# V's global rows copied on VectorE, one values tile fewer, and a rewoven first tile in a windowed-attention and SwiGLU kernel

## The chip, the cores and the metric

The kernel runs on one core of a Trainium2 chip. The metric is the device time of one execution in microseconds (us). The engines are TensorE (PE; its weight loads are listed apart as PEld), VectorE (DVE), ScalarE (ACT), GpSimd (POOL) and SyncE (SP). Each works through its own instructions in program order, and they wait for one another through semaphores. DMA transfers are issued from POOL, SP or ACT and run beside the engines.

## The reference

Attention with a local window and global keys, then a SwiGLU block. There are 4 batches, 8 heads, 768 positions, head size 64, 8 global keys and a window of 96.

```python
scores = scale * np.matmul(q, k.transpose(0, 1, 3, 2))
is_global = pos[None, :] < 8
is_local = (rel >= 0) & (rel < 96)              # rel = query position - key position
keep = is_global | is_local
dist = np.where(is_global & ~is_local, 96.0, np.abs(rel))
scores = np.where(keep, scores - slopes[:, None, None] * dist, -1e9)
a = softmax(scores)
x = np.matmul(a, v)                             # then heads side by side: 3072 x 512
# SwiGLU: d_model 512, d_ff 1536
g = x @ w_gate
out = (g * sigmoid(g) * (x @ w_val)) @ w_out
```

## The kernel before

Keys are taken in chunks of 120 beside the 8 global keys, so that a chunk fills 128 rows: rows 0 to 7 hold the global keys, rows 8 to 127 the chunk's own. `vS0` to `vS3` hold V of the four batches in that form, seven chunks each. A batch's 768 queries are worked in two halves of 384 (`TB`); each half becomes one tile of the SwiGLU block (`t` = 0 to 7). Half 0 of batch 0 needs chunks 0 to 2 and the first 24 keys (`cut`) of chunk 3. For these 24 keys the kernel before has a tile of its own, `vCut`, whose other rows are zero.

```python
vSs = [sb.tile([128, NCH, H, D], FP16, name=f"vS{b}") for b in range(B)]
...
for b in range(B):
    nc.vector.memset(vSs[b][:, 6, :, :], 0.0)
cut = TB - 3 * KC                                   # 24
vCut = sb.tile([128, H, D], FP16, name="vCut")
nc.vector.memset(vCut, 0.0)
...
def copy_globals(b):                                # global rows into all seven chunks, by DMA
    nc.sync.dma_start(
        out=vSs[b][0:NG],
        in_=vG[:, b, :, :].unsqueeze(1).broadcast_to([NG, NCH, H, D]))

def load_v_rest(b, c):                              # a chunk's own rows; casts to fp16 (L171)
    n = min(KC, S - KC * c)
    nc.gpsimd.dma_start(
        out=vSs[b][NG:NG + n, c, :, :],
        in_=v[b, :, KC * c:KC * c + n, :].rearrange("h p d -> p h d"))
```

A quad is four heads. `weigh` makes the denominators (with ones) or the numerators (with V) of a half in one PSUM bank (L447):

```python
def weigh(self, half, dst, side):
    parts = self.parts(half)
    for i, (c, cb, col, o, n) in enumerate(parts):
        vals = vCut if (b, half, c) == (0, 0, 3) else vSs[b][:, c]
        for j in range(4):
            nc.tensor.matmul(
                dst[r, o:o + n],
                lhsT=ones[:, 0:32] if side is None else vals[:, 4 * g + j, side::2],
                rhs=pairs[b, 2 * g + j // 2].at[cb][:, j % 2, col:col + n], ...)
```

The start of the program, in its order:

```python
for c in range(3):
    load_v_rest(0, c)
nc.gpsimd.dma_start(
    out=vCut[NG:NG + cut], in_=v[0, :, 3 * KC:TB, :].rearrange("h p d -> p h d"))
...                                                 # warm-up, first transposes, biases
V(out=vG[:, 0], in_=vG32)
copy_globals(0)
nc.sync.dma_start(out=vCut[0:NG], in_=vG[:, 0])
load_w(wg, 0)
load_half(1, 0, 4)
load_w(wv, 0)
load_half(1, 4, 8)
load_w(wg, 4)
load_w(wv, 4)
for c in range(3, NCH):
    load_v_rest(0, c)
load_w(wg, 8)
load_w(wv, 8)
load_wo(0)
...                                                 # further loads
p_sc(0, 0)                                          # scores of half 0
...
quads[0, 0].denominators(single("den", "x2"))
p_sc(3, 1, "x0", "x1")
for side, tag in enumerate(("a0", "a1")):
    quads[0, 0].numerators(side, single("num", tag))
quads[0, 1].denominators(single("den", "o0"))
for side, tag in enumerate(("x2", "x0")):
    quads[0, 1].numerators(side, single("num", tag))
```

Tile 0 of the SwiGLU block then runs between the parts of half 1's attention. `(f, 0)` is a gate product of 128 columns of d_ff (four matmuls, L555, then tanh on ScalarE and a product on VectorE), `(f, 1)` a value product (four matmuls, then a product on VectorE). `trh` transposes half 1's keys and queries of two pairs of heads, `sch` makes a pair's biases, scores and exponentials, `va` and `vas` the numerators. Four banks `a0` to `a3` hold the first four gates, and then the biases and scores; the spare banks `x0` to `x2` go round. Some operations of VectorE and ScalarE are put into a list, `later`, and taken from it one at a time.

```python
first_gates(0, 2)                                   # matmuls of gates 0 to 3, contraction chunks 0, 1
trh(0, 1, A)()
first_gates(2, 3)
first_gates(3, 4)
tile0 = [(0, 0), (1, 0), (2, 0), (3, 0), (0, 1), (1, 1), sch(0),
         (2, 1), (3, 1), sch(1), trh(2, 3, V), (4, 0), (5, 0), sch(2), (4, 1), (5, 1),
         (6, 0), (6, 1), sch(3), (7, 0), (7, 1), va(0, 0, 1), (8, 0), (8, 1), va(0, 1, 1)]
```

Of the kernel before, what the change touches and what calls it, by code (L numbers as in the profile page):

```python
# [10 lines left out]
FP16 = mybir.dt.float16  # L11
# [4 lines left out]
KC = 120  # L16
WIN = 216
# [3 lines left out]
def _build_dist(S, NG, NL):  # L21


    row = np.arange(128)[:, None]
    col = np.arange(WIN)[None, :]
    key = row - NG
    rel = col - key
    local = (rel >= 0) & (rel < NL) & (key >= 0)
    inner = np.where(local, rel, FAR)
    inner = np.where((row < NG) & (col < KC), NL, inner)  # L30
    first = np.where(local, rel, FAR)
    first = np.where(~local & (key >= 0) & (key < NG) & (col < KC), NL, first)
    d = np.concatenate([first, inner, inner[:, :168], inner[:, :48]], axis=1)
    return d.astype(np.float16)


# [1 line left out]
def kernel(  # L38
# [12 lines left out]
    nc = tc.nc  # L51

    B, H, S, D = q.shape
    NG, NL = int(n_global), int(n_local)
# [7 lines left out]
    NC = DM // 128  # L62
    J = S // 128
    NCH = 7
    TB = 384
# [24 lines left out]
    sb = ctx.enter_context(tc.tile_pool(name="sb", bufs=1))  # L90
# [18 lines left out]
    vG32 = sb.tile([NG, H, D], FP32, name="vG32")  # L109
    nc.sync.dma_start(out=k32, in_=half_of(k, 0, 0, 2))  # L110
    nc.scalar.dma_start(out=ident, in_=const_dr.ap()[:, 0:128])
    nc.scalar.dma_start(out=dist[:, 0:2 * WIN], in_=const_dr.ap()[:, 128:128 + 2 * WIN])
    nc.sync.dma_start(out=q32, in_=half_of(q, 0, 0, 2))
    nc.sync.dma_start(out=vG32, in_=v[0, :, 0:NG, :].rearrange("h p d -> p h d"))
    nc.sync.dma_start(out=dist[:, 2 * WIN:], in_=const_dr.ap()[:, 128 + 2 * WIN:])

    def load_half(half, h0, h1):
        for st, src in ((k16, k), (q16, q)):
# [14 lines left out]
    for b in range(B):  # L133
        nc.vector.memset(vSs[b][:, 6, :, :], 0.0)
    cut = TB - 3 * KC
    vCut = sb.tile([128, H, D], FP16, name="vCut")
    nc.vector.memset(vCut, 0.0)

    slopeI = sb.tile([128, H, 128], FP16, name="slopeI")

# [41 lines left out]
                out=dst.rearrange("p b h d -> p (b h) d"),  # L182
                in_=src[1:, :, 0:NG, :].rearrange("b h p d -> p (b h) d"))

    def copy_globals(b):
        nc.sync.dma_start(
            out=vSs[b][0:NG],
            in_=vG[:, b, :, :].unsqueeze(1).broadcast_to([NG, NCH, H, D]))


    def load_rows(b, i, h):
# [228 lines left out]
    class Quad:  # L420
# [19 lines left out]
        def weigh(self, half, dst, side):  # L440
            b, g = self.b, self.g
            parts = self.parts(half)
            for i, (c, cb, col, o, n) in enumerate(parts):
                vals = vCut if (b, half, c) == (0, 0, 3) else vSs[b][:, c]
                for j in range(4):
                    r = slice(32 * j, 32 * j + 32)
                    nc.tensor.matmul(  # L447
                        dst[r, o:o + n],
                        lhsT=ones[:, 0:32] if side is None else vals[:, 4 * g + j, side::2],
                        rhs=pairs[b, 2 * g + j // 2].at[cb][:, j % 2, col:col + n],  # L450
                        start=(i == 0), stop=(i == len(parts) - 1),
                        skip_group_check=True)
# [55 lines left out]
    def both_values(b, half):  # L508
        two = [quads[b, g] for g in range(2)]
        for quad in two:  # L510
            den = spare("den")
            quad.weigh(half, den, None)
            quad.invert(den)
        srcs = {}
        for g, quad in enumerate(two):
            for side in range(2):
                num = bank("num")
                quad.weigh(half, num, side)
                src = sb2.tile([128, TB], FP32, name="ns", tag="ns", bufs=4)
                nc.scalar.copy(out=src, in_=num[:, 0:TB])  # L520
                srcs[g, side] = src

        def scale_num(eng, g, side):
            eng.tensor_mul(two[g].x_out(half, side), srcs[g, side], two[g].rb)  # L524

        def spread_first():
            two[0].spread()
            for side in range(2):
                scale_num(nc.gpsimd, 0, side)

        later.append(spread_first)
        def spread():
            two[1].spread()

        later.append(spread)
        for side in range(2):
            def scale(side=side):
                scale_num(nc.vector, 1, side)

            later.append(scale)  # L540
# [5 lines left out]
    def products(t, f, which, c0, c1, dst=None):  # L546
        if f == 0 and which == 0 and c0 == 0:
            hTs[t] = sb2.tile([128, NFF, TB], FP16, name="hT", tag="hT", bufs=3)
        if c0 == 0:
            if dst is None:  # L550
                dst = spare("gv"[which] + "ps")
            gv[f, which] = dst
        w = (wg, wv)[which]
        for c in range(c0, c1):
            nc.tensor.matmul(  # L555
                gv[f, which][:, 0:TB], lhsT=w[:, c, 128 * f:128 * f + 128],
                rhs=x_of(t)[:, c, :],
                start=(c == 0), stop=(c == NC - 1))

    def gate_or_val(t, f, which, c0=0):  # L560
        products(t, f, which, c0, NC)
        dst = gv.pop((f, which))

        if which == 0:
            th = sb2.tile([128, TB], FP32, name="th", tag="th")
            nc.scalar.activation(out=th, in_=dst[:, 0:TB], func=AF.Tanh, scale=0.5)  # L566
            if t == 0 and f < 4:
                sl = sb2.tile([128, TB], FP32, name="sl", tag="ns", bufs=4)
            else:
                sl = sb2.tile([128, TB], FP32, name="sl", tag="sl")  # L570
            nc.vector.scalar_tensor_tensor(  # L571
                out=sl, in0=th, scalar=1.0, in1=dst[:, 0:TB], op0=AluOp.add, op1=AluOp.mult)
            gv["sl", f] = sl
        else:
            nc.vector.tensor_mul(hTs[t][:, f, :], dst[:, 0:TB], gv.pop(("sl", f)))  # L575
# [37 lines left out]
    for c in range(3):  # L613
        load_v_rest(0, c)
    nc.gpsimd.dma_start(
        out=vCut[NG:NG + cut], in_=v[0, :, 3 * KC:TB, :].rearrange("h p d -> p h d"))

    warm = single("warm", "o0")

# [37 lines left out]
        make_slope(nc.vector.tensor_scalar_mul, h)  # L657
    p_tr(1, "x2", "o0", A)
    V(out=vG[:, 0], in_=vG32)
    copy_globals(0)  # L660
    nc.sync.dma_start(out=vCut[0:NG], in_=vG[:, 0])
    load_w(wg, 0)
    load_half(1, 0, 4)
    load_w(wv, 0)
# [41 lines left out]
    def first_gates(c0, c1):  # L706
        for f in range(4):
            products(0, f, 0, c0, c1, hb[f])
# [17 lines left out]
    def va(b, g, half):  # L726
        return lambda: quads[b, g].values(half, bank, nc.vector)

    def vas(b, half):
        return lambda: both_values(b, half)  # L730
# [4 lines left out]
    def trh(h0, h1, last):  # L735
        def step():
            b0, b1 = single("trs", "o0", FP16), spare("trs", FP16)
            (a, b), (c, d) = [(t[:, 0:TB], t[:, TB:2 * TB]) for t in (b0, b1)]
            pair_of = [(h0, (c, a)), (h1, (d, b))]
            for hp, tr in pair_of:  # L740
                pairs[0, hp].turn_half(1, tr)
            for hp, tr in pair_of:
                pairs[0, hp].copy_half(1, tr, V, A if hp == h0 else last)
        return step

    def sch(hp):
        def step():
            p = pairs[0, hp]
            scs = [p.bias(1, 0), p.bias(1, 1)]
            for which in range(2):  # L750
                p.scores_half(1, which, scs[which], which == 1 and hp != 1)
        return step
# [9 lines left out]
    def first(t, b):  # L762
        return {(t, 2): [tr(b, 0), tr(b, 1)],
                (t, 4): [sc(b, (0, 0), (0, 1), (1, 0))],
                (t, 5): [tr(b, 2), tr(b, 3)],
                (t, 6): [sc(b, (1, 1), (2, 0), (2, 1))],
                (t, 8): [sc(b, (3, 0), (3, 1))],
                (t, 9): [va(b, 0, 0)],
                (t, 10, 1): [va(b, 1, 0), lambda: run_later(len(later))]}
# [11 lines left out]
    def second(t, b):  # L781
        return {(t, 0): [sc(b, (0, 2), (1, 2))], (t, 3): [sc(b, (2, 2), (3, 2))],
                (t, 7): [vas(b, 1)]}

    first_gates(0, 2)
    trh(0, 1, A)()
    first_gates(2, 3)
    first_gates(3, 4)
    tile0 = [(0, 0), (1, 0), (2, 0), (3, 0), (0, 1), (1, 1), sch(0),
             (2, 1), (3, 1), sch(1), trh(2, 3, V), (4, 0), (5, 0), sch(2), (4, 1), (5, 1),  # L790
             (6, 0), (6, 1), sch(3), (7, 0), (7, 1), va(0, 0, 1), (8, 0), (8, 1), va(0, 1, 1)]

    def ff(t, f0, f1, n_out=(0,)):
        return [(t, f, n_out[(f - f0) % len(n_out)]) for f in range(f0, f1)]

    stretches = [
        (ff(0, 9, 10) + ff(0, 10, 12, (1,)), {}),
        (ff(1, 0, 4, (1, 0, 0, 1)) + ff(1, 4, 10, (1,)) + ff(1, 10, 12, (2,)), first(1, 1)),
        (ff(2, 0, 12, (1,)) + ff(3, 0, 12, (1,)), both(2, 1)),
        (ff(4, 0, 12, (1,)) + ff(5, 0, 12, (1,)), both(4, 2)),  # L800
        (ff(6, 0, 12, (1,)), second(6, 3)),
# [49 lines left out]
    for item in tile0:  # L851
        if callable(item):
            take([item])
            continue
        f, which = item
        run_later(1)
        gate_or_val(0, f, which, NC if f < 4 and which == 0 else 0)
        for fn in after.pop((0, f, which), []):
            fn()

# [60 lines left out]
```

## Time and profile before

| | |
|---|---|
| device time, median of 3 runs | 242.91 us (242.16 to 243.01) |
| span of the profiled execution | 240.4 us |
| TensorE busy | 233.6 us |
| VectorE busy | 167.0 us |
| ScalarE busy | 127.7 us |
| GpSimd busy | 94.0 us |
| moved by DMA | 25.10 MB |

The busy times show which engine has the least room. A wait is listed with the engine and line that waited, what released it, the total in us, how often, and the longest. The timeline lists instructions by start and length; in brackets stands the idle time before one and what ended it. Lines that begin with L are lines of the kernel before: L171 loads a chunk of V, L186 copies global rows by DMA, L447 makes numerators and denominators, L555 the gate and value products, L571 the product after the tanh, L347 the biases and L358 the scores of batch 0.

### The profile page before, as it was taken

Reading aid. Unit: us, or ns where it says so; the run is one execution under the profiler, and the core shown is the slowest. Engines: PE = TensorE matmul, PEld = TensorE weight load, DVE = VectorE, ACT = ScalarE, POOL = GpSimd, SP = SyncE. Lnnn points to the kernel's source line nnn. Section 1 sums busy time; section 2 is a strip of 40 time slices with the busy share of each in tenths; the row PEclk is TensorE's granted clock in tenths of the full one; section 3 lists DMA queues with packets and bytes.
Section 4 is the critical chain, followed back from the end, with each engine's and each line's share of the span. In section 5 each row is a group of like instructions: output and inputs, shape, how many; then the busy total and the mean of one; then the engine's idle time right before and its main releaser. Section 6 shows DMA issues by size and latency. Waiting matters only on the chain.

```text
span 240.4 us, 6040 instructions
## 1 busy us (share of the span) xinstructions
PE 233.6 (97%) x2424; PEld 135.5 (56%) x2424; DVE 167.0 (69%) x362; ACT 127.7 (53%) x288; POOL 94.0 (39%) x113
## 2 busy tenths in 40 slices
PE   7979999999999999999999999999999999999994
PEld 4554665656555556555555556555655556555543
DVE  6687669878897668777786668776785668555530
ACT  4826767887855374376355374376356435233311
POOL 8976574757970002995072252700031223000000
PEclk9999999999999999999999999999999999999999
DMA  7999999999996537999129749930110110111022
GB/s 144 171 200 201 182 204 205 196 165 160 153 140 103 134 80 122 111 136 122 44 57 104 128 109 131 118 64 0 48 44 3 44 44 3 46 44 45 2 88 87
DMA packets 83524, 25.10 MB, mean 104 GB/s; under 512 B 72752, under 2 KB 80552, under 8 KB 83496
## 3 DMA queue, kind: packets, MB, share of 16 engines
q0 software_dynamic: 64208, 14.05, 66.2%
q1 hardware_dynamic: 18856, 10.39, 17.6%
q8 instruction: 19, 0.31, 0.5%
q10 hardware_dynamic: 432, 0.27, 0.4%
q14 instruction: 9, 0.07, 0.1%
HBM read 28.67 MB, written 6.29 MB: 145 GB/s over the span
## 4 chain that ended last, share of the span: by engine, by line
PE 90%; POOL 4%; DMA 3%; ACT 1%; DVE 1%; issue 0%; ACTq 0%; POOLq 0%
PE gps L555 26%; PE vps L555 25%; PE ops L587 25%; PE sc L387 3%; PE num L447 3%; DMA q<-in_q_dram 3%; PE den L447 2%; PE trs L274 1%; POOL vS L171 1%; PE ops L603 1%; POOL k L119 1%; PE sc L347 1%; PE sc L358 1%; DVE sl L571 1%; ACT th L566 1%; PE trs L300 1%
## 5 line engine op out<-in xcount | busy, mean ns | idle before, releaser
L571 DVE SCALAR_TENSOR_TENSOR sl<-th,gps 128x384 f32<-128x384 f32 x96 | 52.7, 552 | 37.3 <-ACT th L566 36.6
L566 ACT ACTIVATE th<-gps 128x384 f32<-128x384 f32 x96 | 47.4, 495 | 58.7 <-PE gps L555 52.8
L555 PE MATMUL vps<-xT,wv 128*128 128x384 f16 x384 | 77.9, 326 | 0.2 <-DMA wv<-in_moe_w_val_dram 0.2
L555 PE MATMUL gps<-xT,wg 128*128 128x384 f16 x384 | 77.9, 327 | 0.0
L587 PE MATMUL ops<-wo,hT 128*128 128x512 f16 x276 | 73.3, 379 | 0.0
L575 DVE TENSOR_TENSOR hT<-vps,sl 128x384 f16<-128x384 f32 x96 | 53.1, 554 | 9.6 <-PE vps L555 1.3
L555 PEld LDWEIGHTS <-wg 128*128 128x128 f16 x384 | 35.4, 98 | 31.1 <-issue 1.6
L555 PEld LDWEIGHTS <-wv 128*128 128x128 f16 x384 | 37.2, 98 | 25.8 <-DMA wv<-in_moe_w_val_dram 0.9
L587 PEld LDWEIGHTS <-hT 128*128 128x128 f16 x276 | 26.9, 98 | 23.5
L395 ACT ACTIVATE at<-sc 128x432 f16<-128x432 f32 x72 | 33.9, 532 | 10.8 <-PE sc L387 10.8
L524 POOL TENSOR_TENSOR xT<-ns,rb 128x384 f16<-128x384 f32 x10 | 9.8, 994 | 66.6 <-DVE rb L463 55.7
L171 POOL DMA_DIRECT2D vS<-in_v_dram x28 | 24.7, 898 | 5.4 <-DMA wo<-in_moe_w_out_dram 1.5
L593 ACT ACTIVATE osb<-ops 128x512 f32<-128x512 f32 x23 | 13.7, 598 | 13.8 <-PE ops L587 13.6
L406 POOL TENSOR_TENSOR at<-at,masks 128x864 f16<-128x864 f16 x4 | 7.3, 1822 | 23.9 <-ACT at L395 19.3
L406 DVE TENSOR_TENSOR at<-at,masks 128x864 f16<-128x864 f16 x20 | 12.2, 609 | 5.2 <-ACT at L395 5.2
L194 POOL DMA_DIRECT2D kst<-in_k_dram x16 | 14.1, 897 | 2.9 <-DMA vS<-in_v_dram 1.8
L194 POOL DMA_DIRECT2D qst<-in_q_dram x16 | 13.8, 890 | 0.2 <-issue 0.2
L369 ACT ACTIVATE at<-sc 128x432 f16<-128x432 f32 (+2 forms) x32 | 11.3, 458 | 3.4 <-PE sc L358 3.4
L520 ACT COPY ns<-num 128x384 f32<-128x384 f32 x20 | 8.1, 493 | 9.3 <-PE num L447 9.3
L447 PE MATMUL num<-at,vS 128*32 128x216 f16 (+6 forms) x560 | 11.2, 226 | 1.2 <-DMA vS<-vG 1.2
L403 DVE TENSOR_TENSOR at<-at,masks 128x432 f16<-128x432 f16 x24 | 8.1, 378 | 4.0 <-ACT at L395 4.0
L457 DVE STREAM_TRANSPOSE dT<-den 128x384 f32<-128x384 f32 x16 | 9.3, 580 | 1.6 <-PE den L447 1.0
(69 smaller groups left out, 167.9 us busy)
## 6 DMA issues: line engine op xcount, KB each, us to landing
out_dram<-osb SPq DMA_DIRECT2D x23, 256.0 KB
vS<-in_v_dram POOLq DMA_DIRECT2D x24, 120.0 KB, 5.4
wg<-in_moe_w_gate_dram POOLq DMA_DIRECT2D x6, 256.0 KB, 7.7
wv<-in_moe_w_val_dram POOLq DMA_DIRECT2D x6, 256.0 KB, 7.8
wo<-in_moe_w_out_dram POOLq DMA_DIRECT2D x4, 384.0 KB, 10.0
qst<-in_q_dram POOLq DMA_DIRECT2D x16, 96.0 KB, 4.2
kst<-in_k_dram POOLq DMA_DIRECT2D x16, 90.0 KB, 4.6
kst<-in_k_dram POOLq DMA_DIRECT2D x2, 384.0 KB, 11.7
```

The costliest lines, as they stand in the source:

```text
L171: nc.gpsimd.dma_start(out=vSs[b][NG:NG + n, c, :, :], in_=v[b, :, KC * c:KC * c + n, :].rearrange("h p d -> p h d"))
L194: nc.gpsimd.dma_start(out=st[b][p0:p0 + n, h // 2, :, h % 2, :], in_=src[b, h, 0:n * J].rearrange("(t p) d -> p t d", p=n))
L369: nc.scalar.activation(out=at[:, hi, 0:col + n], in_=sc[hi][:, 0:col + n], func=AF.Exp, scale=scale)
L395: nc.scalar.activation(out=at[:, hi, :], in_=sc[hi][:, 0:BANK], func=AF.Exp, scale=scale)
L406: mul_eng.tensor_mul(at, at, m[:, :, o:o + BANK])
L447: nc.tensor.matmul(dst[r, o:o + n], lhsT=ones[:, 0:32] if side is None else vals[:, 4 * g + j, side::2], rhs=pairs[b, 2 * g + j // 2].at[c ...
L555: nc.tensor.matmul(gv[f, which][:, 0:TB], lhsT=w[:, c, 128 * f:128 * f + 128], rhs=x_of(t)[:, c, :], start=(c == 0), stop=(c == NC - 1))
L566: nc.scalar.activation(out=th, in_=dst[:, 0:TB], func=AF.Tanh, scale=0.5)
L571: nc.vector.scalar_tensor_tensor(out=sl, in0=th, scalar=1.0, in1=dst[:, 0:TB], op0=AluOp.add, op1=AluOp.mult)
L575: nc.vector.tensor_mul(hTs[t][:, f, :], dst[:, 0:TB], gv.pop(("sl", f)))
L587: nc.tensor.matmul(ops, lhsT=hTs[t][:, f, 128 * i:128 * i + 128], rhs=wo[:, f, :], start=(f == 0), stop=(f == NFF - 1))
L593: nc.scalar.mul(out=osb, in_=ops, mul=0.5)
```

## The change

The change has four parts. The global rows of V go into chunks 0 to 3 of batch 0 by a copy on VectorE, and by DMA into chunks 4 to 6 only. `vCut` is dropped: the 24 keys are loaded into `vS0`'s chunk 3, which is set to zero first, and half 0 reads that chunk. The order of tile 0 is woven anew, with the biases of pair 0 and the first half of two value products between the gates, and half 1's numerators in one group (`vas`) instead of two. The distance table is loaded without its repeated last part, which is copied on VectorE. The aim is to spare the numerators a wait for a DMA copy, to fill gaps of TensorE and to load less at the start.

```diff
-    d = np.concatenate([first, inner, inner[:, :168], inner[:, :48]], axis=1)
+    d = np.concatenate([first, inner], axis=1)
...
-    nc.scalar.dma_start(out=dist[:, 0:2 * WIN], in_=const_dr.ap()[:, 128:128 + 2 * WIN])
+    nc.scalar.dma_start(out=dist[:, 0:2 * WIN], in_=const_dr.ap()[:, 128:])
...
-    nc.sync.dma_start(out=dist[:, 2 * WIN:], in_=const_dr.ap()[:, 128 + 2 * WIN:])
...
-    vCut = sb.tile([128, H, D], FP16, name="vCut")
-    nc.vector.memset(vCut, 0.0)
+    nc.vector.memset(vSs[0][:, 3, :, :], 0.0)
...
-    def copy_globals(b):
+    def copy_globals(b, c0=0):
         nc.sync.dma_start(
-            out=vSs[b][0:NG],
-            in_=vG[:, b, :, :].unsqueeze(1).broadcast_to([NG, NCH, H, D]))
+            out=vSs[b][0:NG, c0:],
+            in_=vG[:, b, :, :].unsqueeze(1).broadcast_to([NG, NCH - c0, H, D]))
...
-                vals = vCut if (b, half, c) == (0, 0, 3) else vSs[b][:, c]
+                vals = vSs[b][:, c]
...
-                scale_num(nc.gpsimd, 0, side)
+                scale_num(nc.gpsimd if b > 0 else nc.vector, 0, side)
...
     nc.gpsimd.dma_start(
-        out=vCut[NG:NG + cut], in_=v[0, :, 3 * KC:TB, :].rearrange("h p d -> p h d"))
+        out=vSs[0][NG:NG + cut, 3], in_=v[0, :, 3 * KC:TB, :].rearrange("h p d -> p h d"))
...
     V(out=vG[:, 0], in_=vG32)
-    copy_globals(0)
-    nc.sync.dma_start(out=vCut[0:NG], in_=vG[:, 0])
+    V(out=vSs[0][0:NG, 0:4], in_=vG[:, 0].unsqueeze(1).broadcast_to([NG, 4, H, D]))
+    copy_globals(0, 4)
     load_w(wg, 0)
...
+    def bias_of(hp, which): ...      # the biases of half 1 for one pair, one score group
+    def scores_of(hp): ...           # the scores onto these biases, and the exponentials
+    def first_val(f):
+        return lambda: products(0, f, 1, 0, 2)      # value product f, contraction chunks 0, 1
+
+    V(out=dist[:, 2 * WIN:2 * WIN + 168], in_=dist[:, WIN:WIN + 168])
+    V(out=dist[:, 2 * WIN + 168:], in_=dist[:, WIN:WIN + 48])
     first_gates(0, 2)
-    trh(0, 1, A)()
     first_gates(2, 3)
     first_gates(3, 4)
-    tile0 = [(0, 0), (1, 0), (2, 0), (3, 0), (0, 1), (1, 1), sch(0),
-             (2, 1), (3, 1), sch(1), trh(2, 3, V), (4, 0), (5, 0), sch(2), (4, 1), (5, 1),
-             (6, 0), (6, 1), sch(3), (7, 0), (7, 1), va(0, 0, 1), (8, 0), (8, 1), va(0, 1, 1)]
+    tile0 = [(0, 0), (1, 0), (2, 0), (3, 0), trh(0, 1, A), bias_of(0, 0), first_val(0),
+             first_val(1), bias_of(0, 1), (0, 1), (1, 1), scores_of(0), (2, 1),
+             trh(2, 3, V), sch(1), (3, 1), sch(2), (4, 0), (5, 0), (4, 1), (5, 1),
+             (6, 0), (6, 1), sch(3), (7, 0), (7, 1), (8, 0), vas(0, 1), (8, 1)]
...
-        (ff(1, 0, 4, (1, 0, 0, 1)) + ff(1, 4, 10, (1,)) + ff(1, 10, 12, (2,)), first(1, 1)),
+        (ff(1, 0, 6, (1, 0, 0, 1, 1, 2)) + ff(1, 6, 10, (1, 1, 1, 0)) + ff(1, 10, 12, (2,)), first(1, 1)),
...
-        gate_or_val(0, f, which, NC if f < 4 and which == 0 else 0)
+        gate_or_val(0, f, which, (NC if f < 4 else 0, 2 if f < 2 else 0)[which])
```

More of the change, by code (lines that the diff above doesn't have):

```diff
@@ L783, in second, with bias_of, step, scores_of @@
                 (t, 7): [vas(b, 1)]}
+    def bias_of(hp, which):
+        def step():
+            pairs[0, hp].sc[1, which] = pairs[0, hp].bias(1, which)
+        return step
+    def scores_of(hp):
+        def step():
+            for which in range(2):
+                pairs[0, hp].scores_half(1, which, pairs[0, hp].sc[1, which], which == 1)
+        return step
+    def first_val(f):
+        return lambda: products(0, f, 1, 0, 2)
+    V(out=dist[:, 2 * WIN:2 * WIN + 168], in_=dist[:, WIN:WIN + 168])
+    V(out=dist[:, 2 * WIN + 168:], in_=dist[:, WIN:WIN + 48])
     first_gates(0, 2)
-    trh(0, 1, A)()
     first_gates(2, 3)
     first_gates(3, 4)
-    tile0 = [(0, 0), (1, 0), (2, 0), (3, 0), (0, 1), (1, 1), sch(0),
-             (2, 1), (3, 1), sch(1), trh(2, 3, V), (4, 0), (5, 0), sch(2), (4, 1), (5, 1),
-             (6, 0), (6, 1), sch(3), (7, 0), (7, 1), va(0, 0, 1), (8, 0), (8, 1), va(0, 1, 1)]
+    tile0 = [(0, 0), (1, 0), (2, 0), (3, 0), trh(0, 1, A), bias_of(0, 0), first_val(0),
+             first_val(1), bias_of(0, 1), (0, 1), (1, 1), scores_of(0), (2, 1),
+             trh(2, 3, V), sch(1), (3, 1), sch(2), (4, 0), (5, 0), (4, 1), (5, 1),
+             (6, 0), (6, 1), sch(3), (7, 0), (7, 1), (8, 0), vas(0, 1), (8, 1)]
     def ff(t, f0, f1, n_out=(0,)):
```

## The prediction

> **What bounds the kernel now.** I read the busy times first, then the waits of TensorE, then a table of stretches over the first 46 us, then the timeline around the longest TensorE gap. The busy line:
>
> ```profile
> PE 233.6 (97%) x2424; PEld 135.5 (56%) x2424; DVE 167.0 (69%) x362; ACT 127.7 (53%) x288; POOL 94.0 (39%) x113
> ```
>
> TensorE is busy for 233.6 of 240.4 us, so 6.8 us of idle time is all that an order of instructions can win. The table of stretches (us from the start; length; then busy us of each engine) says where it lies:
>
> ```profile
> 0.00:1.19 1.19, 0.00 (x0) 0.00 (x1) 0.33 (x3) 0.00 (x0) 0.20 (x4) 1.00 0.00 0
> ...
> 4.00:12.23 8.23, 7.54 (x120) 4.46 (x120) 5.37 (x20) 6.01 (x18) 8.23 (x12) 1.00 1.66 165
> 12.23:13.40 1.17, 0.01 (x2) 0.04 (x2) 1.01 (x3) 0.80 (x3) 1.17 (x2) 1.00 1.24 197
> ...
> 16.40:17.54 1.14, 1.01 (x25) 0.73 (x25) 1.04 (x4) 0.00 (x0) 0.87 (x2) 1.00 1.26 207
> 17.54:22.09 4.55, 4.23 (x37) 2.24 (x34) 4.07 (x13) 2.84 (x7) 3.04 (x4) 1.00 1.41 198
> 22.09:46.00 23.91, 23.91 (x297) 14.44 (x297) 17.88 (x40) 16.74 (x43) 14.21 (x20) 1.00 1.41 197
> ```
>
> From 22.09 us on TensorE has no gap in this table; the rest is the start, the early loads (0.69 us), a gap of 1.16 us at 12.23, some 0.45 us up to 22.09, and the tail. TensorE's waits name the one large gap:
>
> ```profile
> PE num L447 <- DMA vS<-vG: 1.2, 1, 1.2
> ...
> PE vps L555 <- DMA wv<-in_moe_w_val_dram: 0.2, 1, 0.2
> ```
>
> It is the copy of V's eight global rows by DMA, which the first numerators need. Now the lines on which my prediction rests, from the timeline:
>
> ```profile
> 13.40 0.43 PE L447 MATMUL num<-at,vS 128*32 128x216 f16 x12 [1.16 <-DMA vS<-vG]
> ...
> 13.80 0.20 PE L447 MATMUL num<-at,vCut 128*32 128x24 f16 x4
> ...
> 18.45 0.95 POOL L171 DMA_DIRECT2D vS<-in_v_dram  x1 [0.57 <-DMA wv<-in_moe_w_val_dram]
> ```
>
> Half 0 of batch 0 reads V chunks 0 to 2 and 24 keys of chunk 3. For chunk 3 it reads a tile of its own, `vCut`, at 13.80. The full chunk 3 is issued only at 18.45, as the first of the loop over chunks 3 to 6, and the view of that line in that stretch gives its landing:
>
> ```profile
> DMA to landing us min/median/max: 9.4/9.4/9.4
> ```
>
> So the full chunk lands at 18.45 + 9.4 = 27.85 us.
>
> **What the skill says.** (1) The Trainium skill, "DMA: Bandwidth & Descriptors", section "Two DMAs through the same engine are not ordered": the only order that a kernel has on a transfer is its completion semaphore. So whoever reads bytes that a transfer ahead in program order writes must wait for its landing. The trace agrees: the numerators stood 1.16 us for a transfer written ahead of them. They did not stand for the loads of chunks 3 to 6, which also stand ahead in the program and write the same tile `vS0`; so waits go by region, not by tile. (2) "TensorE: Matmul & The Clock Gate", section "Part 1: The HAM clock gate": after an idle window of about 3.4 us the array runs at half rate, and about as much sustained work wakes it. The trace agrees on a cold start: the twelve first matmuls of 256 columns took 2.72 us (1.19 to 3.91), 0.89 ns a column; four warm gate matmuls of 384 columns take 0.65 us, 0.42 ns a column. (3) "VectorE: DVE Perf Modes", section "Side-by-side: where the cycles go for N=2048 bf16": a copy of 2048 16-bit elements is about 693 ns in the 4x mode, 2293 in the plain one. No row here has that copy.
>
> **The change part by part.**
>
> *V's global rows on VectorE.* This removes the wait of 1.16 us: the copy starts after the cast (7.30 + 0.40 = 7.70) and ends by about 8.4, by the page's figure. VectorE was idle for 0.99 us before its next work at 8.70, so it is hidden.
>
> *`vCut` replaced by `vS0` chunk 3.* This is the part that I think decides. The numerators of half 0 now read `vS0[:, 3]`. In program order the loop that loads the full chunk 3 (rows 8 to 127) stands before the first scores, and the diff doesn't touch it. The reads come after that write in program order and overlap it, so they must wait for the landing at 27.85. The weights of the other rows are zero there, but nothing in the program says so. TensorE works in order, so it stops at the first chunk-3 matmul. It gets there at 12.23 (end of the scores) plus 0.40 for the twelve chunk 0 to 2 matmuls, 12.63. The loads do not depend on TensorE, so they run on as before.
>
> *Fewer bytes.* 54 KB of distances, 32 KB of the `vS` copy and 8 KB of `vCut` go: 94 KB, at the 200 GB/s of the table some 0.4 us at most. I take 0.3 us, so chunk 3 lands at 27.55, and with 0.15 us to the release TensorE restarts at R = 27.7.
>
> *From the restart to the scores of pair 0.* Before, from the first `vCut` matmul (13.80) to that point (22.09) was 8.29 us. After, in steps: the rest of the numerators took 1.22 warm (13.80 to 15.02), cold by estimate 1.6: R+1.6. Eight gate matmuls at half rate, 8 x 0.32 = 2.6: R+4.2. The second quad's scaled values were ready 3.76 us after 13.80 (17.56), so they are ready about here too. Eight more gate matmuls, warm by now, 1.3: R+5.5. Then the four gates' tanh and product chain: before, it ended 2.44 us after the gates (18.85 to 21.29), the first two 1.26 us after. The 24 transposes (0.69) fill part of this; then 0.57 of waiting, the first bias 0.25, the partial values 0.65, 0.28 of waiting, the second bias 0.34, the rest of two values 0.65, scores 0.41. Sum: gates + 3.84 = R+9.34 = 37.04. Against 22.09 this is **+14.95 us**.
>
> *The woven order of tile 0 further on.* Transposes move ahead of pair 1, and pair 2's scores follow pair 1's with one value product (0.65) between. Four exponentials take 1.52 us on ScalarE; pair 1's values, scores and biases hide most, and I get 0.35 us of waiting for a bank. Values 4 and 5 then follow their gates directly, while ScalarE still has exponentials: a second 0.35. **+0.7**.
>
> *The burst of half 1.* Same matmuls. VectorE gets in one piece sl 0.55, two inversions 1.6, two spreads 1.16, four scalings 2.04, hT 0.5: 5.85 us. Tile 1 begins 2 x 0.42 + 4 x 0.61 for the burst, 7 x 0.65 of products and 2 x 0.65 of output later, 9.1 us. 3 us to spare: **0**. The two distance copies on VectorE are small and feed masks made after 35 us: **0**. Output parts in tile 1 only change place.
>
> *Given back later.* Short load waits further on (0.4 us before the transposes at 46) vanish, as loads are then 15 us ahead: **-0.45**.
>
> Sum: 14.95 + 0.7 - 0.45 = 15.2; 242.91 + 15.2 = 258.1, **258 us**.
>
> **The rivals.** (a) *No wait on chunk 3*, if the read is somehow not held. Then the gain is what the author wanted: 1.16 us at 12.63, less about 0.7 us as VectorE's scaled values become what the second gates wait for, plus perhaps 0.3 from fewer early bytes, less the 0.7 in the woven order: 242 to 243 us. For it speaks that such a stall would be seen at once by whoever made the change; against it, that `vCut` exists in the kernel before and has no other use than to spare this wait. (b) *The wait, but no cold clock*: then the restart is some 1.3 us shorter, about 256.5. (c) *The wait, and a clock that stays cold longer* because the restart is broken by waits: another 8 gate matmuls and the transposes at half rate, 2 us more, 260. (d) *VectorE's copy in the plain mode*, 2.3 us: keys of pairs 2 and 3 late by about 1.3 us; within the stall it costs nothing, without it it would eat (a)'s gain.
>
> **Range and chances.** (b) and (c) give 256 to 260, the landing is uncertain by 0.5 us, and the restart chain by 1.5: 254 to 262. About one in ten for (a), which is within 2% (4.9 us). All the idle time of TensorE that could go is some 3 us, so faster by over 2% is next to excluded.
>
> **What would show it.** Right: a TensorE wait of about 15 us, from 12.6 to 27.7, by the V load of L171's chunk 3 ahead of a `num` matmul; no `vS<-vG` wait in the first 20 us; LDWEIGHTS and gate matmuls longer for about 4 us after it; the same steady state shifted by 15 us; TensorE's sum of busy time up by 1 to 3 us. Wrong: numerators through at about 14 us. Then the whole sum falls away, and (a) holds.

## The result and the profile after

The changed kernel takes 259.4 us (median of 4 runs, 258.66 to 260.2) against 242.91 us: a ratio of 1.0687, 95% interval 1.0646 to 1.0727. It is slower by some 16.5 us; 258 us was predicted, with 254 to 262 as the range.

In the page of the changed kernel the busy line, the row of TensorE in 40 slices of 6.4 us, and the row of the granted TensorE clock stand like this:

```profile
PE 235.7 (92%) x2424; PEld 136.4 (53%) x2424; DVE 168.0 (65%) x365; ACT 127.4 (50%) x288; POOL 93.9 (36%) x113
...
PE   7800799999999999999999999999999999999994
...
PEclk9965599999999999999999999999999999999999
```

TensorE's share fell from 97 to 92% of a longer span. Two slices are empty, the third and the fourth; there and in the fifth the clock stands at 5 or 6 tenths. All later slices look as before. TensorE's waits, in us in total, times, longest:

```profile
PE num L445 <- DMA vS<-in_v_dram: 14.7, 1, 14.7
...
PE gps L553 <- DVE hT L573: 0.4, 1, 0.4
PE vps L553 <- DVE sl L569: 0.3, 1, 0.3
PE den L445 <- DVE sl L569: 0.3, 1, 0.3
...
PE den L445 <- DVE hT L573: 0.2, 1, 0.2
```

The wait for `vS<-vG` is gone, and a wait for a load of V from memory has taken its place. It is twelve times as long. The four short waits, for products of VectorE, are new too. The timeline of TensorE around the long one:

```profile
12.42 0.43 PE L445 MATMUL num<-at,vS 128*32 128x216 f16 x12
27.51 0.72 PE L445 MATMUL num<-at,vS 128*32 128x24 f16 x20 [14.66 <-DMA vS<-in_v_dram]
...
28.57 1.18 PE L445 MATMUL num<-at,vS 128*32 128x216 f16 x32
29.68 3.96 PE L553 MATMUL gps<-xT,wg 128*128 128x384 f16 x16
```

The twelve matmuls of chunks 0 to 2 run; the first of chunk 3 (24 columns) starts 14.66 us later. The load it stood for, on GpSimd's timeline, and then that line's landing time in the same stretch:

```profile
18.21 0.95 POOL L169 DMA_DIRECT2D vS<-in_v_dram  x1 [0.57 <-DMA wv<-in_moe_w_val_dram]
```

```profile
DMA to landing us min/median/max: 9.3/9.3/9.3
```

18.21 + 9.3 = 27.51: TensorE goes on when the full chunk 3 has landed. When it stopped, at 12.85, that load had not even been issued.

A table of stretches shows where the 16.9 us of the span (240.4 to 257.3) come in. The columns are start and end, length, and the busy us of TensorE, its weight loads, VectorE, ScalarE and GpSimd; then granted clock, DMA share and GB/s. The changed kernel, cut at the stop, at the restart, at the first matmul after half 1's scores of pair 0, and at batch 1's first transposes:

```profile
12.85:27.51 14.66, 0.00 (x0) 0.00 (x1) 0.68 (x2) 0.43 (x3) 9.80 (x13) 0.58 1.51 192
27.51:37.30 9.79, 9.59 (x133) 5.88 (x133) 7.06 (x20) 2.66 (x7) 5.92 (x8) 0.76 1.32 202
37.30:63.50 26.20, 24.84 (x301) 14.72 (x297) 18.59 (x42) 16.85 (x43) 19.18 (x24) 1.00 1.69 160
63.50:257.30 193.80, 190.59 (x1852) 109.44 (x1851) 132.86 (x267) 98.88 (x215) 47.20 (x50) 1.00 0.53 72
```

The kernel before, from the same two last points on:

```profile
22.02:46.16 24.14, 24.14 (x301) 14.51 (x298) 18.02 (x41) 16.97 (x43) 14.44 (x20) 1.00 1.41 197
46.16:240.40 194.24, 190.94 (x1852) 109.76 (x1851) 132.88 (x267) 98.92 (x215) 61.45 (x68) 1.00 0.72 85
```

TensorE is past the scores of pair 0 at 37.30 and not at 22.02: +15.28. The rest of tile 0 and the start of tile 1 take 26.20 and not 24.14: +2.06. From there on 193.80 and not 194.24: -0.44. The sum is 16.90. (The prediction and the expectations set the kernel before at 22.09, where the last score itself ends, and so have 2.13 for 2.06.)

### The profile page after: what moved, and what is told of

It reads as the page before. It is cut to its first block, busy times and chain, and to the rows that moved or that the text cites. A ratio compares the mean times of both kernels' runs of the same rounds, so it can differ in the third digit from the quotient of the medians.

```text
span 257.3 us, 6040 instructions
## 1 busy us (share of the span) xinstructions
PE 235.7 (92%) x2424; PEld 136.4 (53%) x2424; DVE 168.0 (65%) x365; ACT 127.4 (50%) x288; POOL 93.9 (36%) x113
## 4 chain that ended last, share of the span: by engine, by line
PE 82%; DMA 6%; POOL 4%; DVE 3%; ACT 3%; issue 1%; DVEq 0%; ACTq 0%; POOLq 0%
PE gps L553 24%; PE ops L585 23%; PE vps L553 23%; DMA vS<-in_v_dram 4%; PE num L445 3%; PE sc L385 3%; DMA wv<-in_moe_w_val_dram 3%; PE den L445 2%; ACT at L367 2%; DVE sl L569 1%; PE trs L272 1%; POOL vS L169 1%; PE ops L601 1%; POOL k L118 1%; ACT th L564 1%; POOL q L118 1%
## 5 line engine op out<-in xcount | busy, mean ns | idle before, releaser
L553 PE MATMUL gps<-xT,wg 128*128 128x384 f16 x384 | 78.9, 331 | 0.4 <-DVE hT L573 0.4
L553 PEld LDWEIGHTS <-wg 128*128 128x128 f16 x384 | 36.0, 99 | 32.7 <-issue 3.3
L445 PE MATMUL num<-at,vS 128*32 128x216 f16 (+6 forms) x576 | 11.8, 232 | 14.7 <-DMA vS<-in_v_dram 14.7
L445 PEld LDWEIGHTS <-vS 128*32 128x32 f16 x576 | 10.1, 99 | 15.1 <-DMA vS<-in_v_dram 14.9
L518 ACT COPY ns<-num 128x384 f32<-128x384 f32 x24 | 9.8, 493 | 10.4 <-PE num L445 10.4
L503 DVE TENSOR_TENSOR xT<-num,rb 128x384 f16<-128x384 f32 x4 | 2.1, 554 | 14.3 <-PE num L445 14.2
```

The costliest lines, as they stand in the source:

```text
L445: nc.tensor.matmul(dst[r, o:o + n], lhsT=ones[:, 0:32] if side is None else vals[:, 4 * g + j, side::2], rhs=pairs[b, 2 * g + j // 2].at[c ...
L553: nc.tensor.matmul(gv[f, which][:, 0:TB], lhsT=w[:, c, 128 * f:128 * f + 128], rhs=x_of(t)[:, c, :], start=(c == 0), stop=(c == NC - 1))
```

## The experiments

The theory was that one thing makes nearly all of the loss: numerators that read a region to which a load standing ahead in the program still has to write. The main rivals were that the VectorE copy or the new order carries it, or that sharing the tile costs in any case. All ratios below are to the kernel before, measured anew beside each group of runs (medians 242.47 to 242.91 us), with 95% intervals. The start alone differs between executions: in the traces of the experiments the first numerators, or the matmuls put ahead of them, begin between 12.06 us (e1) and 12.95 us (e3). So differences under 1 us are read from stretches of the traces, beside the medians.

| kernel | median us | ratio | interval |
|---|---|---|---|
| changed | 259.4 | 1.0687 | 1.0646 to 1.0727 |
| e1: tile of its own again | 243.62 | 1.0025 | 1.0003 to 1.0047 |
| e2: chunk 3 loaded early | 243.81 | 1.0031 | 1.0011 to 1.0052 |
| e9: loads written later in the text | 244.02 | 1.0054 | 1.0033 to 1.0076 |
| e4: clock kept up through the wait | 258.04 | 1.062 | 1.0567 to 1.0672 |
| e3: new order alone | 245.01 | 1.0072 | 1.0034 to 1.0109 |
| e7: as e1, values in two groups | 242.42 | 0.9995 | 0.9975 to 1.0015 |
| e5: copies and fewer bytes alone | 242.57 | 0.9984 | 0.9963 to 1.0005 |
| e6: as e1, tile 0 woven up to the first scores only | 241.87 | 0.9956 | 0.9938 to 0.9974 |
| e8: as e6, key transposes earlier | 241.91 | 0.9973 | 0.9956 to 0.9991 |
| e10: as e9, order of e6 | 241.99 | 0.9973 | 0.9953 to 0.9992 |

### Three ways to take the wait away

**e1** gives the 24 keys their own tile back.

```diff
-    nc.vector.memset(vSs[0][:, 3, :, :], 0.0)
+    vCut = sb.tile([128, H, D], FP16, name="vCut")
+    nc.vector.memset(vCut, 0.0)
...
-                vals = vSs[b][:, c]
+                vals = vCut if (b, half, c) == (0, 0, 3) else vSs[b][:, c]
...
-        out=vSs[0][NG:NG + cut, 3], in_=v[0, :, 3 * KC:TB, :]...
+        out=vCut[NG:NG + cut], in_=v[0, :, 3 * KC:TB, :]...
...
+    V(out=vCut[0:NG], in_=vG[:, 0])
```

> The changed kernel with one part undone: half 0 reads the 24 keys of chunk 3 from a tile of their own again (its global rows copied on VectorE too). Theory (the numerators wait for the full chunk 3): the TensorE wait of 14.7 us ahead of a numerator is gone, and the half-speed matmuls after it; what is left is the rewoven order, so 243 to 245 us. Rival (the VectorE copy or the rewoven order carries the loss): 255 us or more.

Measured 243.62 us. TensorE's timeline in e1:

```profile
12.06 0.43 PE L446 MATMUL num<-at,vS 128*32 128x216 f16 x12
12.32 0.19 PE L446 MATMUL num<-at,vCut 128*32 128x24 f16 x4
12.35 0.42 PE L446 MATMUL num<-at,vS 128*32 128x216 f16 x12
```

The chunk-3 matmuls follow at once. The VectorE copy is still in, and so is the whole new order, so neither carries the 16 us.

**e2** leaves the tile shared but loads the full chunk 3 as the fourth load of V, ahead of the weights.

```diff
-    for c in range(3):
+    for c in range(4):
         load_v_rest(0, c)
-    nc.gpsimd.dma_start(
-        out=vSs[0][NG:NG + cut, 3], in_=v[0, :, 3 * KC:TB, :]...)
...
-    for c in range(3, NCH):
+    for c in range(4, NCH):
         load_v_rest(0, c)
```

> The changed kernel with the full chunk 3 of V loaded as the fourth load of V, in place of the 24 keys and ahead of the weights; the read stays in the shared tile. Theory (the stop lasts until the landing, whenever that is): chunk 3 is issued at about 7 us and, with the 5.4 us of the other three, lands at about 12.6; the wait falls from 14.7 us to under 0.7 us, and the later loads move back by some 0.5 us: 243 to 246 us. Rival (reading the shared tile is in itself what stops it, through the later loads into that tile): still a wait of 10 us or more, 255 us or more.

Measured 243.81 us. The full chunk lands at about 12.7 us, and all that is left of the stop is this wait of the weight loads (PEld's timeline in e2):

```profile
12.75 0.33 PEld L444 LDWEIGHTS <-vS 128*32 128x32 f16 x20 [0.29 <-DMA vS<-in_v_dram]
```

The stop lasts until the landing, whenever that is.

**e9** changes no instruction. The block of loads that begins with chunk 3 is written behind half 0's numerators. GpSimd works only through loads at that time, so each engine keeps the same instructions in the same order, as the two traces confirm; what changes is which side of the overlap comes first in the program.

```diff
-    for c in range(3, NCH):
-        load_v_rest(0, c)
-    load_w(wg, 8)
     ...                                  # and all the loads after it
     quads[0, 1].numerators(side, single("num", tag))   # x2
+    for c in range(3, NCH):
+        load_v_rest(0, c)
+    load_w(wg, 8)
     ...                                  # and all the loads after it
```

> The changed kernel with one block of text moved: the loop that loads chunks 3 to 6, and all loads after it, stand behind the numerators of half 0 in place of ahead of the scores. Each engine has the same instructions in the same order, the tile stays shared. Now the load of the full chunk 3 follows the read and waits for it on GpSimd. Theory (what stops TensorE is that the write stands ahead of the read in the program): the numerators are through at about 14 us, the load is issued at 18.2 us as before, since the read is long over then, and the time is that of the kernel with a tile of its own, 243.2 to 244 us. Rival (sharing the tile costs in either order, through the wait of the load for the read): the load comes later than 19 us or TensorE waits over 1 us for it in half 1's values, 245 us or more.

Measured 244.02 us, 0.02 us above what was expected. TensorE's timeline in e9, and then GpSimd's:

```profile
12.84 0.72 PE L445 MATMUL num<-at,vS 128*32 128x216 f16 x32
```

```profile
18.84 1.87 POOL L169 DMA_DIRECT2D vS<-in_v_dram  x2 [0.85 <-PE gps L553]
```

All 32 numerator matmuls of the first quad run in one piece, on the shared tile. This is the plainest proof of the cause: with the same instruction streams, 15 us hang on the place of one block in the text. The load is issued at 18.84 us, 0.6 later than in the changed kernel. The profile names a gate matmul as its releaser; how much of the 0.6 us is due to the new wait stays open, as the whole start of this run was some 0.4 us late too.

### What the clock costs

**e4** puts 136 matmuls that compute nothing of the result ahead of the first numerators of the changed kernel.

```diff
+    warm[0] = single("warm", "a0")
+    fill(136)                             # 256 columns each
     for side, tag in enumerate(("a0", "a1")):
         quads[0, 0].numerators(side, single("num", tag))
```

> The changed kernel with 136 matmuls of 256 columns that compute nothing of the result, put ahead of the first numerators; they fill the wait (14.5 us at 0.107 us each). Theory (the clock halves in the wait and takes 1.5 us more after it): the wait for the landing stays and ends at about 27.5 us, the sixteen gate matmuls take 2.6 us of work and not 3.9, and the time falls by 1 to 2 us to 257.4 to 258.4. Rival (the whole loss is waiting, the clock costs nothing because VectorE's chain bounds the restart anyway): 259 to 260 us, as the changed kernel.

Measured 258.04 us, 1.4 us under the changed kernel by the medians; the intervals of the two overlap, so the times alone don't part them. The timeline of e4 does:

```profile
12.35 15.02 PE L621 MATMUL warm<-ones 128*128 128x256 f16 x136
27.43 0.90 PE L445 MATMUL num<-at,vS 128*32 128x216 f16 x32
...
29.08 1.47 PE L553 MATMUL gps<-xT,wg 128*128 128x384 f16 x8
31.21 1.46 PE L553 MATMUL gps<-xT,wg 128*128 128x384 f16 x8 [0.65 <-DVE xT L503]
```

The gates' second group is through at 32.60 and not at 33.57, and the scores of pair 0 at 36.32 and not at 37.30. That is 0.98 us earlier, of which 0.08 are an earlier restart (27.43 and not 27.51). From the restart it takes 8.89 us in place of 9.79: the half clock costs 0.90 us. It would cost more, but 0.65 us of what it takes is time in which TensorE would have waited for VectorE's scaled values anyway. Both theories had a share of the truth: the clock costs, and VectorE hides a part of it.

### What the new order costs

**e3** is the kernel before with the new order alone: the new list of tile 0, `vas(0, 1)` with its scalings on VectorE, and the moved output parts of tile 1, as in the change's diff.

> The kernel before with the rewoven order alone (tile 0, half 1's values in one group scaled on VectorE, output parts of tile 1). Theory (the order costs some 2 us between the first scores of half 1 and tile 1, as the trace of the changed kernel shows, and wins up to 0.5 us before them): 244 to 245 us. Rival (the 2 us come from what stood waiting after the stop, the order itself is neutral or wins): 242 to 243 us.

Measured 245.01 us. From the scores of pair 0 (22.43 us) to batch 1's first transposes (48.63 us) e3 takes 26.20 us, the same as the changed kernel and as e1, whose row is:

```profile
21.55:47.75 26.20, 24.84 (x301) 14.72 (x297) 18.58 (x42) 16.85 (x43) 15.85 (x22) 1.00 1.40 197
```

The 2.06 us over the 24.14 us of before belong to the order and have nothing to do with the long wait.

e3 also shows where the 0.44 us given back come from. From batch 1's first transposes to the first denominators after them the kernel before, the changed kernel and e3 take, in this order:

```profile
46.16:65.58 19.42, 19.30 (x207) 11.36 (x207) 15.65 (x33) 16.58 (x39) 15.31 (x20) 1.00 2.11 164
63.50:82.39 18.89, 18.89 (x207) 11.13 (x206) 15.20 (x32) 15.94 (x38) 5.97 (x7) 1.00 0.99 90
48.63:67.52 18.89, 18.89 (x208) 11.13 (x207) 15.19 (x32) 15.95 (x38) 16.37 (x21) 1.00 1.96 155
```

e3 has no long stop and its loads come as in the kernel before, and it gains the same 0.53 us; e5, in the old order, takes 19.41 us. In this stretch the two orders differ in the moved output parts of tile 1. No run moves these alone.

**e7** is e1 with half 1's values in two groups again.

```diff
-             (6, 0), (6, 1), sch(3), (7, 0), (7, 1), (8, 0), vas(0, 1), (8, 1)]
+             (6, 0), (6, 1), sch(3), (7, 0), (7, 1), va(0, 0, 1), (8, 0), (8, 1), va(0, 1, 1)]
```

> The changed kernel with a tile of its own for the 24 keys and half 1's values in two groups as before; all else of the new order stays. Theory (of the 2.13 us the single group costs 1.4, by denominators that wait for a bank and a product that waits behind VectorE's scaling): 1.4 us less than with the group, 242.1 to 242.4 us, and the bias and value waits of 0.9 us stay. Rival (the waits are VectorE's load whatever the grouping): 243.4 to 243.8 us.

Measured 242.42 us, 1.2 us under e1; expected were 1.4. In the traces the stretch takes 25.06 us (22.39 to 47.45), 1.14 less than e1. The wait of a value product of 0.3 us and a stretched group of biases stay. So the 2.06 us split into 1.14 for the single group and 0.92 for the weaving.

Why the single group costs is seen in e1, in TensorE's timeline and then in VectorE's:

```profile
34.33 0.49 PE L446 MATMUL den<-at,ones 128*32 128x72 f16 x20 [0.33 <-DVE sl L570]
34.99 0.49 PE L446 MATMUL den<-at,ones 128*32 128x72 f16 x20 [0.18 <-DVE hT L574]
...
39.19 0.81 PE L554 MATMUL gps<-xT,wg 128*128 128x384 f16 x4 [0.44 <-DVE hT L574]
```

```profile
35.31 0.58 DVE L456 STREAM_TRANSPOSE dT<-den 128x384 f32<-128x384 f32 x1
35.92 0.23 DVE L457 RECIPROCAL dR<-dT 128x12 f32<-128x12 f32 x1
36.26 0.58 DVE L456 STREAM_TRANSPOSE dT<-den 128x384 f32<-128x384 f32 x1
36.88 0.23 DVE L457 RECIPROCAL dR<-dT 128x12 f32<-128x12 f32 x1
37.02 0.52 DVE L462 STREAM_TRANSPOSE rb<-dR 128x384 f32<-128x384 f32 x1
37.65 1.03 DVE L523 TENSOR_TENSOR xT<-ns,rb 128x384 f16<-128x384 f32 x2
38.59 0.55 DVE L574 TENSOR_TENSOR hT<-vps,sl 128x384 f16<-128x384 f32 x1
```

There are three spare banks. The two denominators take those of gate 7 and value 7, which VectorE has only just freed, and gate 10 takes that of value 8. The product `hT` that frees it stands on VectorE behind the inversions, the spread and two scalings, and ends at 39.14; TensorE starts at 39.19.

### What the gains are worth

**e5** is the kernel before with only the copies on VectorE (own tile kept) and the fewer distance bytes.

```diff
-    copy_globals(0)
-    nc.sync.dma_start(out=vCut[0:NG], in_=vG[:, 0])
+    V(out=vCut[0:NG], in_=vG[:, 0])
+    V(out=vSs[0][0:NG, 0:4], in_=vG[:, 0].unsqueeze(1).broadcast_to([NG, 4, H, D]))
+    copy_globals(0, 4)
```

> The kernel before with the copies of V's global rows on VectorE and the fewer distance bytes, its own tile for the 24 keys and its old order. Theory (the 1.16 us saved at the numerators turn into a wait of the next transposes for the queries of half 1, which land at about 16.6 to 16.9 us): the numerators no longer wait, but the transposes do, and only 0.2 to 0.5 us reach the end: 242.2 to 242.6 us. Rival (the whole wait is won): 241.4 to 241.7 us.

Measured 242.57 us; the interval includes 1. The numerators no longer wait, but the next transposes do (e5's timeline):

```profile
16.32 0.36 PE L299 MATMUL trs<-ident,k 128*64 128x128 f16 x6
17.00 0.36 PE L299 MATMUL trs<-ident,q 128*64 128x128 f16 x6 [0.33 <-DMA q<-in_q_dram]
```

TensorE is past the scores of pair 0 at 22.11, and was at 22.02 before. The first numerators start late here (12.75 us), but the transposes wait for the queries of half 1 all the same: the wait has moved.

**e6** is e1 with the new order up to the scores of pair 0, and from there the old one, but for the output parts of tile 1, which stay moved.

```diff
-             first_val(1), bias_of(0, 1), (0, 1), (1, 1), scores_of(0), (2, 1),
-             trh(2, 3, V), sch(1), (3, 1), sch(2), (4, 0), (5, 0), (4, 1), (5, 1),
-             (6, 0), (6, 1), sch(3), (7, 0), (7, 1), (8, 0), vas(0, 1), (8, 1)]
+             first_val(1), bias_of(0, 1), (0, 1), (1, 1), scores_of(0),
+             (2, 1), (3, 1), sch(1), trh(2, 3, V), (4, 0), (5, 0), sch(2), (4, 1), (5, 1),
+             (6, 0), (6, 1), sch(3), (7, 0), (7, 1), va(0, 0, 1), (8, 0), (8, 1), va(0, 1, 1)]
```

> The changed kernel with a tile of its own for the 24 keys, woven only up to the first scores of half 1, and from there in the order of before, with half 1's values in two groups. Theory (the woven start wins 0.54 us, the rest of the new order loses 2.13 us): 242.0 to 242.4 us, and no wait of TensorE above 0.2 us from 22 us to the tail. Rival (the waits come from the start's shifted spare banks and go along with it): 243 us or more.

Measured 241.87 us, 0.9956 of before (0.9938 to 0.9974): faster than both kernels, and 0.13 us below the range expected. From pair 0's scores to batch 1's transposes it takes 24.08 us (before: 24.14), and the next stretch 18.88 in place of 19.42: most of the gain that its trace shows is that of the moved output parts. That the woven start wins 0.54 us, as expected, its trace doesn't show: from the first numerators past the scores of pair 0 it takes 9.48 us (12.86 to 22.34), and e5 in the old order 9.36 (12.75 to 22.11).

**e8** moves the twelve key transposes of pairs 0 and 1 between the gates' two groups, where e6 waits 0.73 us for VectorE.

```diff
     first_gates(0, 2)
+    trh_keys()
     first_gates(2, 3)
...
-    tile0 = [(0, 0), (1, 0), (2, 0), (3, 0), trh(0, 1, A), bias_of(0, 0), ...
+    tile0 = [(0, 0), (1, 0), (2, 0), (3, 0), trh_queries, bias_of(0, 0), ...
```

> As the half woven kernel, with the twelve key transposes of pairs 0 and 1 of half 1 between the first and the second group of gate matmuls, where TensorE otherwise waits 0.7 us for the scaled values. Theory (this wait is free time, and the keys have landed by 16 us): 0.3 us less than the half woven kernel, 241.7 to 242.1 us. Rival (the keys land too late or the gates are then late by as much): no less than the half woven kernel.

Measured 241.91 us: nothing won. From the first numerator past pair 0's scores it takes 9.48 us (12.24 to 21.72), as e6 does. The wait for scaled values fell from 0.9 to 0.4 us, and the biases now wait 0.4 us for the product after the tanh, for which the transposes had been the filling. The expectation failed: the gap was not free time. The waits point to the chain of VectorE and ScalarE as what runs through.

**e10** has e9's place of the loads and e6's order, and no tile of its own.

> The kernel of the moved loads, without a tile of its own, with the half woven order (woven up to the first scores of half 1, from there as before). Theory (both losses of the change undone, its gains kept): 241.6 to 242.2 us, the time of the half woven kernel with a tile of its own, below the kernel before by 0.3 to 0.5%. Rival (the gain of the half woven kernel was chance of the early loads): 242.5 us or more.

Measured 241.99 us, 0.9973 (0.9953 to 0.9992). The shared tile can be kept, if the load is written behind the read.

## Why the prediction was right, and where it was off

- *The stop.* Right in cause, place and length: expected from 12.63 to 27.7 us, measured from 12.85 to 27.51. e1, e2 and e9 each take it away in a different manner. Rival (a), no wait, is out.
- *V's rows on VectorE.* The copy took 0.82 us, not 0.69, and is hidden: VectorE's next work still waited 0.37 us for TensorE. Of the figures of the Trainium skill, "VectorE: DVE Perf Modes", section "Side-by-side: where the cycles go for N=2048 bf16", that of the 4x mode (693 ns) is nearer than that of the plain one (2293 ns), so rival (d) is out.
- *The restart.* Expected 9.34 us, measured 9.79. The numerators took 2.17 us and not 1.6; the sixteen gates 3.89 as summed (2.6 + 1.3); the rest 3.73 and not 3.84. The Trainium skill, "TensorE: Matmul & The Clock Gate", section "Part 1: The HAM clock gate", states the half rate, and the granted clock shows it: 0.50 from 15.06 to 32.14 us. The page's 3.4 us fit less well: the clock fell 2.2 us after TensorE stopped and rose 4.6 us after the restart. (For the cold start the prediction had the durations alone; the clock column reads 1.00 there.) Between (b) and (c), the clock cost 0.90 us (e4), less than the 1.3 by which (b) was set off.
- *The woven order.* Expected +0.7, measured 0.92 (e7 against the kernel before).
- *The burst.* This term failed: 0 was expected, and 1.14 us were measured. The step asked only whether tile 1 would find its input in time (3 us to spare, and it did). It did not follow the three spare banks, whose reuse hangs on the same VectorE queue.
- *Given back later.* Expected -0.45, measured -0.44, but the reason was wrong and the agreement is luck. The prediction let load waits vanish because the loads run 15 us ahead. e3 and e6, without that lead, gain 0.53 and 0.54 us in tile 1, where the output parts moved, a step that the prediction put at nothing. The trace of before has no wait for a load at the transposes at 46; one of 0.42 us stands at 54.34, ahead of weight loads, and e6 still has it (at 55.24).
- *The sum.* 15.2 us expected, 16.9 in the span: 1.14 more for the burst, 0.22 for the weaving, 0.33 up to pair 0's scores. All three were set too low.

## What to carry to other kernels

A small tile for a part of a buffer can look like waste and be what keeps a later full load out of a reader's way. Before it is merged away, follow every write to that region that stands ahead of the read in the program; if one is issued late, split the tile or write the load behind the read. And when work is gathered into one group, count what its queue holds up for the reuse of banks, not only whether its result is in time. A term can also come out right for the wrong reason: the 0.44 us given back were told apart only by a run without the main effect.

## What the runs showed of the hardware

TensorE stood idle from 12.85 to 27.51 us in the changed kernel. The granted clock, the third number from the end of a row, is 0.50 in this stretch, and 1.00 in the 2.21 us ahead of it and in the 1.43 us after it:

```profile
15.06:32.14 17.08, 4.63 (x76) 3.04 (x77) 3.64 (x9) 0.00 (x0) 11.98 (x16) 0.50 1.48 194
```

So the clock fell 2.2 us after the stop and rose 4.6 us after the restart. The sixteen gate matmuls behind the numerators took 3.89 us. With 0.163 us for one at full rate and 0.32 at half, some eight ran at half rate, which agrees. A run of matmuls through the same wait (e4) kept the granted clock at 1.00 and took 15.02 us for 136 of them, 0.110 us each. Filling the wait so won 0.9 us of the restart; taking the wait away won 15.
